# Seven block products per group of an expert: three of them made a group later, the fourth corner added in PSUM, and the first expert's operands built over two earlier blocks

## The chip, the cores and the metric

The kernel runs on one core of one Trainium2 chip. The metric is the device time of one execution in microseconds (us): 1494.73 us is the median of three runs of the kernel before (1494.47 to 1494.83).

## What is computed

Eight sequences of 1856 rows go through an attention-like layer, and its 14848 result rows of 256 numbers through a layer of 16 experts, of which each row takes one. Per row the router picks the best of four groups and the best of four experts in it; the expert is two matrix products with a ReLU between them, 256 to 1024 and back to 256 numbers, and the result is scaled by the product of two softmax weights.

```python
for e in range(Eg):
    h = np.maximum(xg[mask_e] @ w1[g, e], 0.0)
    ye = h @ w2[g, e]
    out[tok_idx] = combined[:, None] * ye
```

## The kernel before

Every matrix product is made from three products of rounded operands: a value is split into a high part (a copy in the matmul's format, made by ScalarE) and a low part (value minus high part, made by VectorE, often through the helper `lows`, L1172), and low times high, high times high and high times low are added up in PSUM.

The first part (until about 800 us) is the attention and the routing; the rows are sorted by expert into a table in device memory. The experts are then taken in order of their number of rows. The first four ("old" experts) run in twelve blocks of at most 512 rows (loop at L1314, `blocks`): `phase1` (L784) makes the 1024 hidden numbers as eight tiles of 128, `phase2_t` (L848) the result; the last two blocks, of 256 and of 512 rows, belong to the fourth expert.

The other twelve experts (loop at L1372) have their rows cut into two halves of w rows, w falling from 512 to 424 with the expert (and 448 for the last). Their first product is made by a block scheme: with both matrices cut in two by two, seven block products and some sums stand for eight block products. `duo_phase1` (L1257) makes four groups g of 128 hidden numbers, and in each the products 1 to 7, each of three matmuls of w columns. Per group:

- Products 1 and 2 go to a bank X (three banks take turns: x0, p0, x0, p1), product 5 to bank W; products 6, 7 and 4 to Y, product 3 to Z (two of Y and of Z, by the group's parity).
- After 1 ScalarE copies X to Y (L1289), after 5 it copies W to a tile in SBUF, `m5_w` (L1292).
- After 6 VectorE writes Z = Y + m5 (L1294). Product 7 then adds on Y, so it waits until this sum has read Y.
- After 7 VectorE makes the fourth corner C22 = Y + m5 in an SBUF tile `c22_w` (L1299). Product 4 adds on Y, so it waits until this has read Y.
- The four corners leave by `evict` (L1277): ScalarE writes the ReLU's high part (L1283), VectorE the low part (L1284, a scalar_tensor_tensor).

The order of the products is written out (L1306 to L1309) and TensorE follows it as written:

```python
seq += [(g, 1), (g, 5)] + [(g - 1, 4)] * (g > 0) + [(g, 6), (g, 2)] + [(g - 1, 3)] * (g > 0) + [(g, 7)]
```

The other engines' orders come from a planner that places the instructions by modelled times, earlier program order first; what is wrapped in `pin` stays behind the instruction that was written just before it on the same engine. Each engine then runs its queue in that order. A tile takes a buffer of its pool when its first writer runs; pool `vb` has 18 buffers, `at` three (L97, L103).

After the products of an expert its result is made in two halves, 48 matmuls each (`phase2_t`, L869). Into these matmuls are woven: the last two products (of the fourth group, 4 and 3, at slots 6 and 9), the "chores" (L1394), which build the next expert's operands (`split_w1` L1174, `split_duo` L1224, loads of weights by SyncE's queue), one each third matmul in the first half and each second in the second, and, late in the second half (slots 12, 14, 18, 20), the next expert's first four products. GpSimd splits the second weight (`split_w2`, L1192) during the products and sends the result rows to memory (L897). Result tiles that were still to be scaled and sent (`unsent`, `finish` L886) are taken up at every third product.

For the first of the twelve (expert 4) there is no expert before it, so its operands are built around the last old block: `split_w1` after that block's `phase1` (L1349), `split_duo` in the middle of its `phase2_t` (L1362). The weight's parts are the tiles p, a, s, t; a, s, t lie in pool `at`, which also holds the old experts' first weight. r0 to r5 are raw operands, r2 and r3 first hold sums of the weight's blocks and are then overwritten by `split_duo` with sums of the rows' blocks; x0 to x6 are the rows' high and low parts. `duo_banks` (L1249) writes four matmuls with the old weight into the Y and Z banks ahead of the first product. The steps of an "overflow" plan (`plan`, L1043, tiles `ov_...`) are strewn over blocks and products, on VectorE.

Of the kernel before, what the change touches and what calls it, by code (L numbers as in the profile page):

```python
# [19 lines left out]
P = 128  # L20
# [9 lines left out]
def tile_glu_attn_moe(  # L30
# [1118 lines left out]
    wst = {}  # L1149

    def duo_tiles():
        role = ["r0", "r1", "x5", "x6", "r2", "r3", "w0", "w1", "w2", "w3", "r4", "r5", "p", "x0", "x1", "x2", "x3", "x4"]
        for r in role:
            wst[r] = (new_vraw if r[0] == "r" else new_vb)(f"duo_{r}")
        for a in ("a", "s", "t"):
            wst[a] = new_at(f"duo_{a}", F32R)
# [17 lines left out]
    def split_w1():  # L1174
# [3 lines left out]
        s1, s3, s2, s4 = r2[:, 0:FH], r2[:, FH:F], r3[:, 0:FH], r3[:, FH:F]  # L1178
        yield pin(nc.vector.tensor_sub(out=s3, in0=a11, in1=a21))
        pin(nc.scalar.copy(out=wst["p"][:, 0:FH], in_=a11))  # L1180
        yield nc.vector.tensor_add(out=s1, in0=a21, in1=a22)
        nc.scalar.copy(out=wst["a"][:, 0:F], in_=r1)
        yield nc.vector.tensor_sub(out=s2, in0=s1, in1=a11)
        nc.scalar.copy(out=wst["s"][:, 0:F], in_=r2)
        yield nc.vector.tensor_sub(out=s4, in0=a12, in1=s2)
        nc.scalar.copy(out=wst["t"][:, 0:F], in_=r3)
        yield lows(wst["p"][:, FH:F], a11, wst["p"][:, 0:FH])
        yield lows(wst["a"][:, F:2 * F], r1, wst["a"][:, 0:F])
        yield lows(wst["s"][:, F:2 * F], r2, wst["s"][:, 0:F])
        yield lows(wst["t"][:, F:2 * F], r3, wst["t"][:, 0:F])  # L1190
# [33 lines left out]
    def split_duo(e):  # L1224
# [11 lines left out]
        nc.scalar.copy(out=wst["x0"][:, both], in_=r5[:, both])  # L1236
        yield nc.vector.tensor_sub(out=r2[:, two], in0=r5[:, two], in1=r4[:, two])
        nc.scalar.copy(out=wst["x3"][:, both], in_=r2[:, both])
        yield nc.vector.tensor_sub(out=r3[:, one], in0=r5[:, two], in1=r2[:, one])
        yield nc.vector.tensor_sub(out=r3[:, two], in0=r5[:, one], in1=r3[:, one])  # L1240
        nc.scalar.copy(out=wst["x5"][:, both], in_=r3[:, both])
        yield lows(wst["x2"][:, 512:512 + w], r4[:, one], wst["x2"][:, one])
        yield lows(wst["x4"][:, both], r2[:, both], wst["x3"][:, both])
        yield lows(wst["x1"][:, both], r5[:, both], wst["x0"][:, both])
        yield lows(wst["x6"][:, both], r3[:, both], wst["x5"][:, both])
# [11 lines left out]
    def duo_phase1(e):  # L1257
# [8 lines left out]
        def product(g, m):  # L1266
# [30 lines left out]
            elif m == 7:  # L1297
                t = sb("zm", [P, 512], F32, 2, f"c22_w{e}_{g}")[:, 0:w]
                nc.vector.tensor_add(out=t, in0=Y, in1=tmp[g])  # L1299
                evict(t, g + NF // 2, 1)  # L1300
            elif m == 3:
                evict(Z, g, 1)
            else:
                evict(Y, g + NF // 2, 0)

        seq = []  # L1306
        for g in range(NF // 2):
            seq += [(g, 1), (g, 5)] + [(g - 1, 4)] * (g > 0) + [(g, 6), (g, 2)] + [(g - 1, 3)] * (g > 0) + [(g, 7)]
        seq += [(NF // 2 - 1, 4), (NF // 2 - 1, 3)]  # L1309
# [4 lines left out]
    for i, (e, r0, n) in enumerate(blocks):  # L1314
# [21 lines left out]
        if e + 1 == NOLD and blocks[i - 1][0] != e:  # L1336
            duo_tiles()
# [176 lines left out]
```

## Time and profile before

| | |
|---|---|
| median of three runs | 1494.73 us |
| the profiled execution, its own time | 1498.23 us |
| its span (first to last instruction) | 1496.4 us |
| granted clock over the span, share of 2.4 GHz | 0.989 |
| TensorE busy | 1435.7 us (96%) |
| VectorE busy | 1253.7 us (84%) |
| ScalarE busy | 1015.7 us (68%) |
| GpSimd busy | 399.8 us (27%) |

Times below are us from the span's start. A matmul's busy time ends where its modelled end is, well after the next one has begun, so matmuls that follow each other closely leave no idle time, and the distance from start to start is their real pace. "Idle before" names the instruction whose end released the waiting one.

### The profile page before, as it was taken

Reading aid. Unit: us, or ns where it says so; the run is one execution under the profiler, and the core shown is the slowest. Engines: PE = TensorE matmul, PEld = TensorE weight load, DVE = VectorE, ACT = ScalarE, POOL = GpSimd, SP = SyncE. Lnnn points to the kernel's source line nnn. Section 1 sums busy time; section 2 is a strip of 40 time slices with the busy share of each in tenths; the row PEclk is TensorE's granted clock in tenths of the full one; section 3 lists DMA queues with packets and bytes.
Section 4 is the critical chain, followed back from the end, with each engine's and each line's share of the span. In section 5 each row is a group of like instructions: output and inputs, shape, how many; then the busy total and the mean of one; then the engine's idle time right before and its main releaser. Section 6 shows DMA issues by size and latency. Waiting matters only on the chain.

```text
span 1496.4 us, 22711 instructions
## 1 busy us (share of the span) xinstructions
PE 1435.7 (96%) x6981; PEld 1223.1 (82%) x6981; DVE 1253.7 (84%) x2460; ACT 1015.7 (68%) x1824; POOL 399.8 (27%) x462
## 2 busy tenths in 40 slices
PE   9999999999999999999999999879999999989996
PEld 7898888887888888887788989657777777878885
DVE  7889999989989999898996676697888987788883
ACT  8897787877878778787763444346666666666662
POOL 0002211222202221022223212144323344443343
PEclk9999999999999999999999999979999999999998
DMA  9988969889798997988864645415444344445441
GB/s 320 330 218 238 239 185 235 206 244 226 199 218 204 252 229 197 222 200 230 198 165 103 142 118 117 102 50 136 115 118 120 105 125 116 122 118 128 119 108 39
DMA packets 400045, 256.48 MB, mean 171 GB/s; under 512 B 244131, under 2 KB 355262, under 8 KB 399920
## 3 DMA queue, kind: packets, MB, share of 16 engines
q1 hardware_dynamic: 387984, 223.97, 60.4%
q0 software_dynamic: 11856, 30.90, 7.0%
q8 instruction: 55, 0.90, 0.3%
q14 instruction: 70, 0.57, 0.1%
q10 hardware_dynamic: 80, 0.13, 0.0%
HBM read 108.29 MB, written 89.21 MB: 132 GB/s over the span
## 4 chain that ended last, share of the span: by engine, by line
PE 71%; DVE 8%; issue 7%; DMA 6%; ACT 3%; POOL 3%; SPq 1%; DVEq 0%; ACTq 0%; POOLq 0%
PE o L403 12%; PE o L404 12%; PE o L406 11%; PE duo_p L869 10%; PE yT L869 6%; PE sc L366 4%; PE sc L367 4%; DMA yr_w<-yp_w 2%; PE ph L792 2%; PE ph L793 2%; PE ph L794 2%; PE duo_y L1275 2%; DVE hl_w L1284 2%; DMA out_dram<-y_w,meta_w 1%; POOL out_dram L897 1%
## 5 line engine op out<-in xcount | busy, mean ns | idle before, releaser
L403 PE MATMUL o<-ah,vl 128*128 128x512 f32 (+2 forms) x960 | 354.5, 370 | 0.6 <-DVE ah L378 0.4
L404 PE MATMUL o<-ah,vh 128*128 128x512 f32 (+2 forms) x960 | 354.3, 369 | 0.0
L406 PE MATMUL o<-al,vh 128*128 128x512 f32 (+2 forms) x896 | 329.1, 369 | 0.2 <-DVE al L356 0.2
L638 POOL DMA_INDIRECT bucket<-rows,di x121 | 137.5, 1136 | 376.1 <-issue 218.3
L370 ACT ACTIVATE r<-sc 128x512 f32<-128x512 f32 (+2 forms) x312 | 178.0, 571 | 66.8 <-PE sc L367 43.4
L403 PEld LDWEIGHTS o<-ah,vl 128*128 128x128 f32 x960 | 180.2, 188 | 30.6 <-DVE ah L378 0.8
L404 PEld LDWEIGHTS o<-ah,vh 128*128 128x128 f32 x960 | 180.2, 188 | 29.1
L381 DVE TENSOR_TENSOR al<-r,ah 128x512 fp32r<-128x512 f32 (+2 forms) x280 | 187.9, 671 | 17.3 <-DVE ah L378 0.5
L406 PEld LDWEIGHTS o<-al,vh 128*128 128x128 f32 x896 | 167.8, 188 | 27.2 <-DVE al L381 0.7
L869 PE MATMUL duo_p<-hh_w,duo_w 128*128 128x496 f32 (+9 forms) x692 | 182.9, 375 | 0.1
L377 ACT ACTIVATE r<-r 128x512 f32<-128x512 f32 (+2 forms) x284 | 173.9, 612 | 9.0
L869 PEld LDWEIGHTS duo_p<-hh_w,duo_w 128*128 128x128 f32 x692 | 129.8, 188 | 17.6 <-POOL duo_w L1199 0.5
L378 DVE CAST ah<-r 128x512 fp32r<-128x512 f32 (+2 forms) x284 | 116.9, 412 | 28.1 <-ACT r L377 22.8
L897 POOL DMA_INDIRECT out_dram<-y_w,meta_w x92 | 95.4, 1037 | 107.9 <-ACT y_w L896 90.9
L366 PE MATMUL sc<-zm,z2h 128*128 128x512 f32 (+2 forms) x312 | 120.5, 386 | 0.2 <-ACT r L370 0.2
L367 PE MATMUL sc<-zm,z2l 128*128 128x512 f32 (+2 forms) x312 | 118.9, 381 | 0.0
L869 PE MATMUL duo_p<-hl_w,duo_w 128*128 128x496 f32 (+9 forms) x346 | 105.3, 375 | 0.0
L306 DVE STREAM_TRANSPOSE mt<-r 128x512 f32<-128x512 f32 x147 | 103.7, 705 | 0.6
L356 DVE TENSOR_TENSOR al<-at,ah 128x512 fp32r<-128x512 f32 (+1 forms) x168 | 94.9, 579 | 1.2 <-ACT ah L355 1.1
L355 ACT CAST ah<-at 128x512 fp32r<-128x512 f32 (+1 forms) x168 | 86.1, 532 | 8.8 <-DMA at<-sym 4.7
L869 PE MATMUL yT<-hh,w_e 128*128 128x512 f32 (+6 forms) x384 | 82.4, 334 | 0.0
L888 DVE COPY y_w<-yr_w 128x512 uint16<-128x512 uint16 x92 | 47.5, 528 | 37.5 <-DMA yr_w<-yp_w 21.3
(239 smaller groups left out, 2893.5 us busy)
## 6 DMA issues: line engine op xcount, KB each, us to landing
sym<-mt SPq DMA_DIRECT2D x126, 256.0 KB
duo_r<-in_w_dram SPq DMA_DIRECT2D x48, 512.0 KB
at<-sym SPq DMA_DIRECT2D x84, 256.0 KB
bucket<-padrow SPq DMA_DIRECT2D x32, 660.0 KB
at<-sym SPq DMA_DIRECT2D x84, 160.0 KB
vr<-in_v_dram SPq DMA_DIRECT2D x23, 512.0 KB
ut<-in_uT_dram SPq DMA_DIRECT2D x23, 512.0 KB
raw_e<-in_w_dram SPq DMA_DIRECT2D x16, 512.0 KB
```

Source lines behind the costliest of these rows:

```text
L366: held(nc.tensor.matmul(ps[:, 0:w], z2h[:, ks], zm, start=True, stop=False))
L367: held(nc.tensor.matmul(ps[:, 0:w], z2l[:, ks], zm, start=False, stop=True))
L370: held(nc.scalar.activation(out=a, in_=ps[:, 0:w], func=AF.Relu, scale=1.0 / S))
L377: held(nc.scalar.activation(out=a, in_=a, func=AF.Square))
L378: held(nc.vector.tensor_copy(out=ah, in_=a))
L381: held(nc.vector.tensor_sub(out=al, in0=a, in1=f32(ah)))
L403: held(nc.tensor.matmul(o, vl[:, dsl], ah, start=(i == 0), stop=False))
L404: held(nc.tensor.matmul(o, vh[:, dsl], ah, start=False, stop=end and al is None))
L406: held(nc.tensor.matmul(o, vh[:, dsl], al, start=False, stop=end))
L638: nc.gpsimd.indirect_dma_start(out=views[(b * NQ + 2 * half + hs[h]) * NT + i], out_offset=bass.IndirectOffsetOnAxis(ap=di[0:n, i0 + i:i0 ...
L869: nc.tensor.matmul(o, wt["2"][f // 2][:, w0:w0 + P], hs[f][q // 2][:, 0:n], start=(at == 0), stop=(at == 3 * NF - 1))
L897: nc.gpsimd.indirect_dma_start(out=outs(), out_offset=bass.IndirectOffsetOnAxis(ap=meta[0:m, t, 1:2], axis=0), in_=y[0:m], in_offset=None, ...
```

## The change

- Product 7 of a group moves behind products 1 and 5 of the next group, product 4 behind that group's 6 and 2, in front of 3. After the last group come 7, 3, 4; the loop makes all but the last one ahead of the result's matmuls, and 4 goes to slot 4 of them.
- C22 is added into bank X of its own group, in PSUM, in place of an SBUF tile, and evicted from there.
- The operands of expert 4 are built earlier: seven of the eight steps of `split_w1` during `phase1` of the last but one old block, eight steps of `split_duo` during `phase1` of the last one, the rest right after it, before the last block's `phase2_t`.
- In `split_w1` the copies of p, a and s move one place forward, and that of t to just before its low part. In `split_duo` the low parts of x2 and x4 come before the second pair of sums, x6's and x0's steps after them, x1's last.
- The tiles are made when they are first asked for, and not all at once.
- `unsent` tiles are taken up only when fewer than 14 products are left; the chores of the first half begin at slot 6 (14 places for 16).

```diff
+        pin(nc.scalar.copy(out=wst["p"][:, 0:FH], in_=a11))
         yield pin(nc.vector.tensor_sub(out=s3, in0=a11, in1=a21))
-        pin(nc.scalar.copy(out=wst["p"][:, 0:FH], in_=a11))
+        nc.scalar.copy(out=wst["a"][:, 0:F], in_=r1)
         yield nc.vector.tensor_add(out=s1, in0=a21, in1=a22)
-        nc.scalar.copy(out=wst["a"][:, 0:F], in_=r1)
+        nc.scalar.copy(out=wst["s"][:, 0:F], in_=r2)
         yield nc.vector.tensor_sub(out=s2, in0=s1, in1=a11)
-        nc.scalar.copy(out=wst["s"][:, 0:F], in_=r2)
         yield nc.vector.tensor_sub(out=s4, in0=a12, in1=s2)
-        nc.scalar.copy(out=wst["t"][:, 0:F], in_=r3)
         yield lows(wst["p"][:, FH:F], a11, wst["p"][:, 0:FH])
         yield lows(wst["a"][:, F:2 * F], r1, wst["a"][:, 0:F])
         yield lows(wst["s"][:, F:2 * F], r2, wst["s"][:, 0:F])
+        nc.scalar.copy(out=wst["t"][:, 0:F], in_=r3)
         yield lows(wst["t"][:, F:2 * F], r3, wst["t"][:, 0:F])
...
         nc.scalar.copy(out=wst["x2"][:, one], in_=r4[:, one])
         yield nc.vector.tensor_sub(out=r2[:, one], in0=r4[:, two], in1=r4[:, one])
-        nc.scalar.copy(out=wst["x0"][:, both], in_=r5[:, both])
         yield nc.vector.tensor_sub(out=r2[:, two], in0=r5[:, two], in1=r4[:, two])
         nc.scalar.copy(out=wst["x3"][:, both], in_=r2[:, both])
+        yield lows(wst["x2"][:, 512:512 + w], r4[:, one], wst["x2"][:, one])
+        yield lows(wst["x4"][:, both], r2[:, both], wst["x3"][:, both])
         yield nc.vector.tensor_sub(out=r3[:, one], in0=r5[:, two], in1=r2[:, one])
         yield nc.vector.tensor_sub(out=r3[:, two], in0=r5[:, one], in1=r3[:, one])
         nc.scalar.copy(out=wst["x5"][:, both], in_=r3[:, both])
-        yield lows(wst["x2"][:, 512:512 + w], r4[:, one], wst["x2"][:, one])
-        yield lows(wst["x4"][:, both], r2[:, both], wst["x3"][:, both])
+        yield lows(wst["x6"][:, both], r3[:, both], wst["x5"][:, both])
+        nc.scalar.copy(out=wst["x0"][:, both], in_=r5[:, both])
         yield lows(wst["x1"][:, both], r5[:, both], wst["x0"][:, both])
-        yield lows(wst["x6"][:, both], r3[:, both], wst["x5"][:, both])
...
             elif m == 7:
-                t = sb("zm", [P, 512], F32, 2, f"c22_w{e}_{g}")[:, 0:w]
-                nc.vector.tensor_add(out=t, in0=Y, in1=tmp[g])
-                evict(t, g + NF // 2, 1)
+                nc.vector.tensor_add(out=X, in0=Y, in1=tmp[g])
+                evict(X, g + NF // 2, 1)
...
-            seq += [(g, 1), (g, 5)] + [(g - 1, 4)] * (g > 0) + [(g, 6), (g, 2)] + [(g - 1, 3)] * (g > 0) + [(g, 7)]
-        seq += [(NF // 2 - 1, 4), (NF // 2 - 1, 3)]
+            seq += [(g, 1), (g, 5)] + [(g - 1, 7)] * (g > 0) + [(g, 6), (g, 2)] + [(g - 1, 4), (g - 1, 3)] * (g > 0)
+        seq += [(NF // 2 - 1, m) for m in (7, 3, 4)]
...
+        if i + 2 == NB:
+            first = {"w1": split_w1()}
+
+        def mid_duo(f):
+            mid(f)
+            if i + 2 == NB and f:
+                next(first["w1"])
+            if last and f % 2:
+                for _ in range(2):
+                    next(first["x"])
+
+        hs = phase1(i, wts[e], x, n, mid_duo, False)
...
         if i + 2 == NB:
             duo_rows(NOLD)
+            first["x"] = split_duo(NOLD)
         if last:
-            for _ in split_w1():
+            for _ in first["w1"]:
                 pass
+            for _ in first["x"]:
+                pass
+            duo_w2(NOLD)
...
-            if last and t == 1:
-                duo_w2(NOLD)
-                for _ in split_duo(NOLD):
-                    pass
...
-        while len(prods) > 2:
+        while len(prods) > 1:
...
-            if unsent and len(prods) % 3 == 0:
+            if unsent and len(prods) < 14 and len(prods) % 3 == 0:
...
-        slots = {(0, 6): [tail[0]], (0, 9): [tail[1]]}
+        slots = {(0, 4): [prods[0]]}
         for d in range(ND):
-            for k in range(0, 24, 3):
+            for k in range(0 if d else 6, 24, 3):
                 slots.setdefault((d, k), []).append(chore(1))
```

## Rows read from the trace of the kernel before

**Rows 1.** The page, its first part: busy time and share of each engine.

```profile
PE 1435.7 (96%) x6981; PEld 1223.1 (82%) x6981; DVE 1253.7 (84%) x2460; ACT 1015.7 (68%) x1824; POOL 399.8 (27%) x462
```

**Rows 2.** The busy times in stretches (windows); columns in the first line.

```profile
core 0: us, PE busy (x) PEld busy (x) DVE busy (x) ACT busy (x) POOL busy (x), PEclk, DMA share, GB/s
...
962.00:993.00 31.00, 15.82 (x35) 10.11 (x36) 27.35 (x39) 9.45 (x14) 14.46 (x11) 0.61 0.32 80
...
1024.40:1441.80 417.40, 392.76 (x1801) 333.80 (x1800) 344.13 (x516) 262.59 (x476) 170.57 (x180) 1.00 0.47 119
...
1468.00:1496.40 28.40, 16.11 (x87) 14.32 (x85) 3.85 (x8) 5.58 (x12) 6.78 (x7) 0.85 0.22 47
```

**Rows 3.** The waits of TensorE from 950 us to the end.

```profile
PE duo_y L1275 <- DVE duo_z L1294: 21.7, 24, 2.0
...
PE duo_y L1275 <- DVE c_w L1299: 8.1, 9, 3.9
...
PE duo_x L1275 <- ACT duo_x L1234: 3.7, 1, 3.7
```

**Rows 4.** The timeline of TensorE at one wait: start, duration, what, idle before.

```profile
1247.96 0.80 PE L1275 MATMUL duo_z<-duo_x,duo_t 128*128 128x464 f32 x3
1250.56 0.90 PE L1275 MATMUL duo_y<-duo_x,duo_s 128*128 128x464 f32 x3 [1.79 <-DVE duo_z L1294]
1251.29 0.80 PE L1275 MATMUL duo_x<-duo_x,duo_p 128*128 128x464 f32 x3
1251.92 0.80 PE L1275 MATMUL duo_w<-duo_x,duo_s 128*128 128x464 f32 x3
```

**Rows 5.** The groups of instructions (lines) from 950 us, VectorE's.

```profile
L1284 DVE SCALAR_TENSOR_TENSOR hl_w<-c_w,hh_w 128x496 fp32r<-128x496 f32 (+9 forms) x36 | 50.5, 1404 | 17.4 <-ACT hh_w L1283 16.5 <-issue 0.6
...
L1284 DVE SCALAR_TENSOR_TENSOR h_w<-c_w,h_w 128x496 fp32r<-128x496 f32 (+9 forms) x12 | 8.8, 732 | 1.9 <-ACT h_w L1283 0.7
...
L1284 DVE SCALAR_TENSOR_TENSOR hl_w<-duo_y,hh_w 128x496 fp32r<-128x496 f32 (+9 forms) x48 | 30.4, 634 | 0.8 <-ACT hh_w L1283 0.8
...
L1299 DVE TENSOR_TENSOR c_w<-duo_y,m_w 128x496 f32<-128x496 f32 (+9 forms) x48 | 30.5, 635 | 1.0 <-PE duo_y L1275 0.5 <-issue 0.3
...
L1294 DVE TENSOR_TENSOR duo_z<-duo_y,m_w 128x496 f32<-128x496 f32 (+9 forms) x48 | 31.2, 649 | 19.5 <-PE duo_y L1275 16.7 <-ACT y_w L896 2.3 <-ACT hh_w L1283 0.4
```

**Rows 6.** The timeline of TensorE between the old blocks and the first products.

```profile
962.13 0.50 PE L1255 MATMUL duo_z<-w1h_e 128*128 128x512 f32 x1 [0.41 <-ACT yp L872]
...
966.33 1.22 PE L1275 MATMUL duo_x<-duo_x,duo_p 128*128 128x512 f32 x2 [3.70 <-ACT duo_x L1234]
...
987.62 1.65 PE L1275 MATMUL duo_y<-duo_x,duo_a 128*128 128x512 f32 x3 [3.92 <-DVE c_w L1299]
...
992.85 0.85 PE L1275 MATMUL duo_y<-duo_x,duo_s 128*128 128x512 f32 x3
```

**Rows 7.** The timeline of ScalarE there.

```profile
962.67 1.04 ACT L1186 CAST duo_t<-duo_r 128x1024 fp32r<-128x1024 f32 x1 [0.59 <-PE duo_z L1255]
```

**Rows 8.** The timeline of VectorE there, and one row ahead of it.

```profile
935.34 1.34 DVE L771 COPY xf<-xp 128x2048 uint16<-128x2048 uint16 x1
...
963.74 1.23 DVE L1172 TENSOR_TENSOR duo_t<-duo_r,duo_t 128x1024 fp32r<-128x1024 f32 x1 [8.12 <-ACT duo_t L1186]
...
964.89 2.60 DVE L1228 COPY duo_r<-xp_w 128x1024 uint16<-128x1024 uint16 x4
...
967.38 0.67 DVE L1235 TENSOR_TENSOR duo_r<-duo_r 128x512 f32<-128x512 f32 x1
...
980.24 3.16 DVE L1111 TENSOR_TENSOR ov_it<-ov_it 128x64 f32<-128x64 f32 x1
```

**Rows 9.** The busy times in the last two old blocks, and in one expert's second part.

```profile
927.50:941.00 13.50, 13.50 (x107) 13.12 (x107) 11.06 (x27) 5.91 (x13) 4.58 (x4) 1.00 0.61 109
...
941.00:953.50 12.50, 12.50 (x56) 10.20 (x55) 8.86 (x17) 5.97 (x10) 4.30 (x5) 1.00 0.24 62
...
1218.60:1239.10 20.50, 20.21 (x96) 17.53 (x95) 19.09 (x29) 12.24 (x19) 1.92 (x3) 1.00 0.42 104
```

More of the change, by code (lines that the diff above doesn't have):

```diff
@@ L1147, in tile_glu_attn_moe, with __missing__ @@
     planned = plan()
[L1149 to L1156, printed above, removed]
+    class Duo(dict):
+        def __missing__(self, k):
+            new = new_vraw if k[0] == "r" else new_vb if k[0] in "xwp" else lambda name: new_at(name, F32R)
+            self[k] = new(f"duo_{k}")
+            return self[k]
+    wst = Duo()
     def duo_w1(e):
@@ L1336, in tile_glu_attn_moe @@
         if e + 1 == NOLD and blocks[i - 1][0] != e:
-            duo_tiles()
             duo_w1(NOLD)
-        hs = phase1(i, wts[e], x, n, mid, False)
+        if i + 2 == NB:
[8 more added lines that the diff above has]
+        hs = phase1(i, wts[e], x, n, mid_duo, False)
         if i + 1 == NEARLY:
@@ L1374, in tile_glu_attn_moe @@
         build2 = split_w2()
-        at = len(prods)
-        while len(prods) > 2:
+        while len(prods) > 1:
             next(build2, None)
@@ L1379, in tile_glu_attn_moe @@
                 next(planned, None)
-            if unsent and len(prods) % 3 == 0:
+            if unsent and len(prods) < 14 and len(prods) % 3 == 0:
                 unsent.pop(0)()
             if more and len(prods) == 8:
-                for _ in build2:
-                    pass
                 duo_w1(e + 1)
@@ L1387, in tile_glu_attn_moe @@
             prods.pop(0)()
-        for _ in build2:
-            pass
-        work = []
+        work = ()
         if more:
-            hs2, prods2 = [], []
             def chores():
@@ L1399, in tile_glu_attn_moe @@
             work = chores()
-        tail = prods
-        half_p = [(0, 6)], [(0, 9)]
-        slots = {(0, 6): [tail[0]], (0, 9): [tail[1]]}
         def chore(n):
             return lambda: [next(work, None) for _ in range(n)] if more else None
+        slots = {(0, 4): [prods[0]]}
         for d in range(ND):
-            for k in range(0, 24, 3):
+            for k in range(0 if d else 6, 24, 3):
                 slots.setdefault((d, k), []).append(chore(1))
```

## The prediction

> **What bounds the kernel now.** I read the page's first part, then busy time in stretches, then TensorE's waits, then the timelines around the largest of them. TensorE is busy 96% of the span [rows 1], so at best the other 4%, and time in which it runs slowly, can be won. The stretches say where that lies [rows 2]: in the ten middle experts TensorE is idle 417.40 - 392.76 = 24.6 us of 417; between the last old block and expert 4's products 15.2 of 31 us, with the granted clock at 0.61, so part of the busy time there is at the lower of the clock's two levels; and in the last 28.4 us, after the last product, which the change hardly touches. The waits put names to it [rows 3]: product 7 waits for the sum Z = Y + m5 24 times, 21.7 us; product 4 for the sum C22 nine times, 8.1 us; what is left is the start of expert 4, where ScalarE's copy of x2 comes 3.70 us late [rows 6].
>
> A wait costs more than its row says. Three matmuls of 464 columns take 0.63 us (1251.29 to 1251.92, [rows 4]). The product at 1250.56 should have begun at 1247.96 + 0.63 = 1248.59, so it is 1.97 late where the row says 1.79, and the next one begins 0.73 instead of 0.63 after it: 2.07 in all, 0.28 over the row.
>
> Why the sums are late, the groups of instructions tell [rows 5]. In one group VectorE makes two sums and four low parts. At 0.634 us each (five of the six forms lie between 0.634 and 0.649) that is 3.8 us in 7 x 0.63 = 4.4 us of TensorE's time, which fits. But C22's low part takes 1.404 us in 36 of its 48 instances; then it is 4.6 us, and VectorE falls behind in every group. Both inputs of this one lie in SBUF; the other low parts read PSUM. In the fourth groups, the 12 others, it takes 0.732. GpSimd splits weights during the products and is nearly idle after them (1.92 of 20.5 us, [rows 9]), so I read the extra 0.77 us as VectorE waiting for GpSimd at SBUF.
>
> **The change part by part.**
>
> *Products 7, 4 and 3 later.* Between 6 and 7 of a group now lie 2, 4, 3, 1, 5 in place of 2 and 3: three products more, 1.9 us, against a longest wait of 2.0 us [rows 3]. Between 7 and 4 lie 6 and 2 where 1 and 5 lay: no more room than before. Between 6 and 3 there is still nearly a whole turn. What can be won is 21.7 + 8.1, less the 3.92 that belongs to expert 4's start [rows 6]: 25.9 in 32 waits, and 32 x 0.28 = 9.0 beside it, 34.9 us.
>
> *C22 in PSUM.* The sum goes from SBUF to PSUM as Z does: 0.635 to 0.649, 48 x 0.014 = 0.7 us more. Its low part then has the form of the others: 36 x (1.404 - 0.634) = 27.7 and 12 x (0.732 - 0.634) = 1.2 us less. VectorE wins 28.2 us, none of it on the path by itself; it is what makes the sum come in time for product 4, which got no more room. The bank X now stays taken until C22 is evicted, and the group after next begins in it: from the sum's end two more steps of 0.634 against two products of slack, a wait of 0 to 0.5 us in one group of an expert, since only x0 comes round within one. A rule speaks against this. By the rows, a low part out of PSUM is no dearer: 0.634 against 0.732 [rows 5]. The Trainium skill, Perfetto Trace Analysis, section Optimizing Scalar/DVE Operations, gives some 60 ns of access overhead per VectorE instruction on SBUF and some 125 on PSUM; by that VectorE would get back 48 x 0.065 = 3 us of its 28, and the forecast would stand.
>
> *Left over in the twelve experts.* Nothing before shows the new waits. Lower bound 0. Upper bound: product 4's waits stay, 4.2 us in eight of the nine plus 8 x 0.28, and the chores, which now begin at slot 6 and so up to six matmuls (1.3 us) later, are late for the next expert's first products by that much in eleven experts, 14 us: 20 in all. That danger is real: in the second part of an expert VectorE is busy 19.09 of 20.50 us [rows 9]. Against it, VectorE now leaves the products without a backlog, and x1, the last operand made, is for the fourth product. I take 6, half a microsecond per expert: 34.9 - 6 = **29 us won**.
>
> *Expert 4's start.* A matmul of 512 columns takes 0.23 us (0.63 / 3 x 512 / 464, [rows 4]). From the end of the last one into the Z bank (962.13 + 0.23) to 992.85 eleven products ran [rows 6]: 33 x 0.23 = 7.6 us of work in 30.5, 22.9 lost. The chain [rows 7, 8]: t's copy waits until the old weight's buffer is free (962.67), its low part follows (963.74), and the row copies L1228, pinned behind it, begin at 964.89; all of x0 to x6 comes after. With the change p, a, s, the row copies, x2, x3 and x4 come out of the last two old blocks, x0 and x1 need only r5 and can come before 962, and products 1 and 5 start at once. But t still waits for 962.67, and r3, which t's low part reads, is what `split_duo` overwrites to make x5 and x6. So product 6 waits for: t's copy 1.04, its low part 1.23 (until 964.97), two sums of 0.67 (966.3), x5's copy 1.04 (967.4), x6's low part 1.23 (968.7; a copy and a low part of that width, priced by t's). Products 1 and 5 end at 963.7, so 6 begins 3.7 us late and its third matmul a second time: 4.9 us. After an idle stretch of 3.70 us the clock was at the lower level before, and after 3.92 the matmuls ran at half pace until 992.85, 5.2 us [rows 2, 6]. I count 2 us for that (between 0 and 2.6). The overflow plan runs on VectorE in that very stretch (one step took 3.16 us, [rows 8]) and is not moved: 0 to 6, I take 3.
>
> *The two old blocks.* They get some 3.9 us of VectorE's work (four steps of 0.67 and a low part of 1.23; a's and the first sum's place can be earlier) in a block where it has 2.4 free, and 5.8 (2.60 for the row copies, three steps of 0.67, 1.23) where it has 3.6 and 2 us of sums leave [rows 8, 9]. The second fits. In the first, the copy that joins the last block's rows (935.34, pinned) slips, and TensorE, without a gap there, waits for it: 0 to 3.5, I take 2. Lost in all 4.9 + 2 + 3 + 2 = 12 of 22.9: **11 us won**.
>
> *At no cost.* `unsent` tiles later: nothing in the products reads them, and GpSimd's weight splits go ahead of their sends, so the result's matmuls find their weights earlier; without that cover a late split would hold the first of them. m5 of two groups lives at once now, and the pool that it shared with C22's tile has the two buffers for it. SyncE: `duo_w2` of expert 4 is issued half a block earlier; its r0 and r1 have been read by then, so it does not hold the block's transposes behind it. The weight splits on GpSimd still wait for the old block's buffers. ScalarE makes as many copies and ReLUs as before and is busy 68% [rows 1].
>
> **The sum.** 1498.23 - 29 - 11 = 1458; that execution's span is 1496.4 and the 1.8 around it stay; the runs' median, 1494.73, lies 3.5 us below it, so 1455 us.
>
> **The rivals.**
> 1. *Everything goes as drawn* (0.60): 1455, between 1445 and 1465.
> 2. *The waits vanish whole* (0.13): no left-over, no plan, no slip: 34.9 + 22.9 - 4.9 = 53 us, 1498.2 - 53 - 3.5 = 1442. For it: VectorE's 28 us; against it, VectorE's 93% in an expert's second part [rows 9].
> 3. *VectorE becomes the bound* (0.13): its queue keeps half of the 34.9, and expert 4's start gives 5: 1498 - 22.5 - 3.5 = 1472.
> 4. *The eviction stays at 1.4 us* (0.07), because its length has another cause than where C22 lies; the change then doesn't do what it says in this part. Product 7 wins by its distance, product 4 keeps its 8.1 + 9 x 0.28 = 10.6: 34.9 - 10.6 - 6 + 11 = 29 us, 1498.2 - 29 - 3.5 = 1466.
> 5. *Slower* (0.04): VectorE's queue, laid out by modelled times, has C22's sum behind the low part of the next group's product 2. Product 4 follows that 2 directly and would wait for a ReLU, a low part and the sum, some 3 x 0.634 = 1.9 us, in 3 groups of 12 experts: 68 us less 40 won, 1495 + 28 = 1523. It decides from 40 / 36 = 1.1 us per group. Against it: 7 comes two products before 2, so the sum is ready first.
>
> The remaining 0.03 is no change. Faster or slower by 0.2%, 3 us, is about what a measurement of this kernel can tell. Faster: 0.60 + 0.13 + 0.13 + 0.07 = 0.93; same 0.03; slower 0.04. The range reaches from rival 2 to rival 3: 1442 to 1473.
>
> **What would show it.** Right: TensorE's waits for Z gone from its list; C22's low part at 0.63 us; products of expert 4 from about 962.5 with one stop before product 6 that ends with x5 and x6; about 38 us from expert to expert at 464 columns. Wrong: waits of product 4 for C22, or of product 2 or 6 for VectorE's low parts, in every expert; TensorE idle between the last two old blocks; a clock below 1.00 after expert 4's start.

## The result and the profile after

The changed kernel takes 1471.87 us (median of four runs, 1469.22 to 1473.58) against 1494.78 for the kernel before on the same chip: ratio 0.9844, 95% interval 0.9827 to 0.9861, 22.9 us faster. The profiled execution took 1471.43 us with a span of 1469.6. The two profiled executions differ by 26.8 us. That splits at three landmarks: the first matmul of the last but one old block, where the change begins, the start of the twelfth product of expert 4, and the start of the last matmul of a product:

```
us                                before   after   won   forecast
up to the last but one old block  927.46   925.59   1.9     0
from there to the 12th product     65.39    55.69   9.7    11
12th to last product              474.61   459.18  15.4    29
last product to the end            28.94    29.14  -0.2     0
```

The first 1.9 us are not shown to be the change's: the edits begin behind that mark, and it lies between 922.5 and 928.2 in the eleven profiled executions with the early operands and between 926.5 and 928.4 in the three without. So the start of expert 4 gave nearly what was drawn and the steady part gave half. The page's first part, then the stretches that answer to [rows 2] (busy us of each engine, clock, DMA):

```profile
PE 1428.8 (97%) x6981; PEld 1229.3 (84%) x6981; DVE 1231.9 (84%) x2460; ACT 1020.1 (69%) x1824; POOL 394.0 (27%) x462
```

```profile
962.00:981.30 19.30, 10.36 (x28) 7.03 (x28) 16.93 (x24) 6.38 (x10) 12.65 (x9) 0.65 0.30 85
1016.00:1419.80 403.80, 390.17 (x1801) 339.89 (x1800) 329.64 (x520) 266.90 (x477) 162.54 (x178) 0.99 0.48 123
```

The ten middle experts take 403.8 us instead of 417.4 with the same 1801 matmuls; TensorE is still idle 13.6 us of them, and the clock is no longer 1.00. TensorE's waits in place of [rows 3] (us in total, times, longest):

```profile
PE duo_y L1274 <- ACT duo_y L1288: 8.3, 11, 1.8
PE duo_y L1274 <- ACT duo_x L1241: 5.9, 1, 5.9
PE duo_p L869 <- POOL duo_w L1198: 3.6, 1, 3.6
PE duo_y L1274 <- DVE duo_p L1297: 3.4, 3, 1.8
PE duo_y L1274 <- DVE duo_x L1171: 1.9, 1, 1.9
```

Code lines lie one lower than before. The waits for Z are gone. In the steady part three others have come: product 6 for ScalarE's X to Y copy (L1288), the second phase for GpSimd's split of the second weights (L1198), product 4 for C22 (L1297). The second and the fifth line are expert 4's start. C22's low part, [rows 5], in VectorE's groups:

```profile
L1283 DVE SCALAR_TENSOR_TENSOR hl_w<-duo_p,hh_w 128x496 fp32r<-128x496 f32 (+9 forms) x36 | 23.1, 641 | 0.5 <-ACT hh_w L1282 0.5
L1283 DVE SCALAR_TENSOR_TENSOR h_w<-duo_p,h_w 128x496 fp32r<-128x496 f32 (+9 forms) x12 | 7.6, 632 | 0.0
```

The lines go by bank, so the first counts product 2's low parts in p0 and p1 with C22's of one group; C22's of the two groups in x0's bank stand with product 2's there, at 0.64. C22's low part is as cheap as the rest. The start of expert 4 against [rows 6 to 8]: TensorE, ScalarE and VectorE in their timelines.

```profile
967.74 1.22 PE L1274 MATMUL duo_y<-duo_x,duo_t 128*128 128x512 f32 x2 [5.93 <-ACT duo_x L1241]
970.90 0.79 PE L1274 MATMUL duo_y<-duo_x,duo_t 128*128 128x512 f32 x1 [1.94 <-DVE duo_x L1171]
```

```profile
961.90 1.05 ACT L1188 CAST duo_t<-duo_r 128x1024 fp32r<-128x1024 f32 x1
966.65 1.04 ACT L1241 CAST duo_x<-duo_r 128x1024 fp32r<-128x1024 f32 x1 [3.70 <-DVE duo_r L1240]
```

```profile
963.81 1.21 DVE L1171 TENSOR_TENSOR duo_t<-duo_r,duo_t 128x1024 fp32r<-128x1024 f32 x1
...
965.92 0.69 DVE L1240 TENSOR_TENSOR duo_r<-duo_r,duo_r 128x512 f32<-128x512 f32 x1
967.42 1.23 DVE L1093 TENSOR_TENSOR ov_big<-ov_le,ov_it 128x1024 f32<-128x1024 f32 x1 [0.80 <-POOL duo_w L1197]
968.56 2.29 DVE L1171 TENSOR_TENSOR duo_x<-duo_r,duo_x 128x1024 fp32r<-128x1024 f32 x1
```

t's copy, its low part, the two sums over r3, x5's copy: the chain of the prediction. Product 6 begins at 967.7 for 967.4, but this execution was 1.9 us ahead when the change began, so it is some 2 us later than drawn. Products 1 and 5 ran inside the old block, before the last matmul into the Z bank (961.42), so they fill nothing of this wait; and a row's copy (963.46) and a row's weighting (964.94) stand among VectorE's steps of the chain. Behind it a plan step (L1093) stands ahead of x6's low part.

**Where the steady part loses.** Twelve times after expert 4's start product 6 comes over 0.3 us late for the copy, 10.4 us in all by start-to-start times. One such place, ScalarE:

```profile
1192.78 0.51 ACT L896 ACTIVATE y_w<-y_w,meta_w 128x256 f32<-128x256 f32 x1
1193.48 0.55 ACT L1291 COPY m_w<-duo_w 128x472 f32<-128x472 f32 x1 [0.18 <-PE duo_w L1274]
1193.93 0.56 ACT L1288 COPY duo_y<-duo_p 128x472 f32<-128x472 f32 x1
```

L896 weights a result row for a send. Behind it the queue has m5's copy, which waits for product 5, ahead of Y's copy, which needs only product 1; product 6 begins at 1194.54, 0.7 late. Seven of the twelve are like this. In three others, the two dearest among them, a send's weighting and the second phase's evictions stand ahead; ScalarE, then VectorE:

```profile
1263.15 0.51 ACT L896 ACTIVATE y_w<-y_w,meta_w 80x256 f32<-80x256 f32 x1 [1.96 <-DVE y_w L888]
1263.56 0.78 ACT L872 COPY yp_w<-duo_p 128x768 uint16<-128x768 uint16 x1
...
1264.43 0.54 ACT L1288 COPY duo_y<-duo_p 128x456 f32<-128x456 f32 x1
```

```profile
1262.61 0.46 DVE L888 COPY y_w<-yr_w 80x512 uint16<-80x512 uint16 x1 [2.29 <-DMA out_dram<-y_w,meta_w]
```

VectorE's copy of the row waits until an earlier send has left its buffer, ScalarE's weighting waits for VectorE, the X to Y copy for ScalarE, and product 6 for the copy. In all twelve a weighting is among the four ScalarE instructions ahead of the copy.

### The profile page after: what moved, and what is told of

Its sections match the earlier page's. It is cut to its first block, busy times and chain, and to the rows that moved or that the text cites. A ratio compares the mean times of both kernels' runs of the same rounds, so it can differ in the third digit from the quotient of the medians.

```text
span 1469.6 us, 22695 instructions
## 1 busy us (share of the span) xinstructions
PE 1428.8 (97%) x6981; PEld 1229.3 (84%) x6981; DVE 1231.9 (84%) x2460; ACT 1020.1 (69%) x1824; POOL 394.0 (27%) x462
## 4 chain that ended last, share of the span: by engine, by line
PE 78%; DVE 10%; issue 5%; DMA 2%; POOL 2%; ACT 2%; SPq 0%; DVEq 0%; ACTq 0%; POOLq 0%
PE o L403 13%; PE o L404 13%; PE o L406 12%; PE duo_p L869 11%; PE yT L869 5%; PE duo_y L1274 4%; PE sc L366 4%; PE sc L367 4%; PE ph L792 2%; PE duo_x L1274 2%; PE ph L793 2%; PE ph L794 2%; PE duo_w L1274 2%; PE duo_p L1274 1%; PE duo_z L1274 1%
## 5 line engine op out<-in xcount | busy, mean ns | idle before, releaser
L406 PEld LDWEIGHTS o<-al,vh 128*128 128x128 f32 x896 | 167.9, 188 | 26.9 <-DVE al L381 0.7
L897 POOL DMA_INDIRECT out_dram<-y,meta x37 | 40.9, 1105 | 130.8 <-DVE y L894 124.9
```

The lines of the kernel that those rows point to most:

```text
L406: held(nc.tensor.matmul(o, vh[:, dsl], al, start=False, stop=end))
L897: nc.gpsimd.indirect_dma_start(out=outs(), out_offset=bass.IndirectOffsetOnAxis(ap=meta[0:m, t, 1:2], axis=0), in_=y[0:m], in_offset=None, ...
```

## The experiments

Each ran at least five times, beside the kernel before on the same chip; chips differ (the kernel before has medians from 1493.75 to 1498.33 us), so the ratios are compared. "Steady" is the time from the twelfth product of expert 4 to the last one, in the profiled execution.

```
                         ratio   95% interval     steady us
changed kernel           0.9844  0.9827 - 0.9861  459.2  (before 474.6)
1  PSUM alone            0.9996  0.9985 - 1.0008  473.6
2  PSUM and order        0.9889  0.9871 - 0.9907  458.6
3  sends early           0.9850  0.9831 - 0.9868  456.9
4  x5 in r4              0.9782  0.9764 - 0.9800  459.1
5  C22 in SBUF           0.9893  0.9876 - 0.9910  467.7
6  weighting on VectorE  0.9891  0.9876 - 0.9905  468.6
7  weighting on GpSimd   1.0023  1.0011 - 1.0035  481.4
8  3 ahead of 6          1.0022  1.0009 - 1.0035  492.1
9  no sends between      0.9736  0.9722 - 0.9749  446.2
10 plan later            0.9830  0.9817 - 0.9844  464.6
11 sends behind 6        0.9810  0.9797 - 0.9824  460.4
12 weighting split       0.9908  0.9889 - 0.9928  478.1
```

**1. C22 in PSUM alone.** In the kernel before:

```
-                t = sb("zm", [P, 512], F32, 2, f"c22_w{e}_{g}")[:, 0:w]
-                nc.vector.tensor_add(out=t, in0=Y, in1=tmp[g])
-                evict(t, g + NF // 2, 1)
+                nc.vector.tensor_add(out=X, in0=Y, in1=tmp[g])
+                evict(X, g + NF // 2, 1)
```

> The kernel before with one part of the change alone: C22 added in the PSUM bank X instead of in an SBUF tile; order of the products, sends and expert 4's start stay as before. Theory (the prediction's): VectorE's 1.4 us low parts of C22 are what makes the sums late, so product 7's 21.7 us of waits for Z and product 4's 8.1 us fall by more than half: 1480 us (1474 to 1485). Rival: the two products between 6 and 7 are too short a distance for the sum whatever VectorE's load is: the waits for Z stay above 15 us and the time is 1489 us or more. In both the low part of C22 takes 0.63 us.

No change at all, though VectorE's busy time falls from 1253.7 [rows 1] to 1231.6 us. TensorE's waits, then VectorE and TensorE at one of them:

```profile
PE duo_y L1275 <- DVE duo_x L1298: 14.7, 13, 4.3
PE duo_y L1275 <- DVE duo_z L1294: 5.8, 8, 1.5
PE duo_y L1275 <- DVE duo_p L1298: 5.0, 4, 1.4
```

```profile
1298.21 2.15 DVE L888 COPY y_w<-yr_w 80x512 uint16<-80x512 uint16 x1
1300.26 0.62 DVE L1284 SCALAR_TENSOR_TENSOR hl_w<-duo_x,hh_w 128x456 fp32r<-128x456 f32 x1
1300.80 0.61 DVE L1284 SCALAR_TENSOR_TENSOR hl_w<-duo_z,hh_w 128x456 fp32r<-128x456 f32 x1
1301.34 0.62 DVE L1298 TENSOR_TENSOR duo_x<-duo_y,m_w 128x456 f32<-128x456 f32 x1
```

```profile
1302.02 0.68 PE L1275 MATMUL duo_y<-duo_x,duo_a 128*128 128x456 f32 x2 [1.84 <-DVE duo_x L1298]
```

The waits for Z fell as the theory said, 21.7 to 5.8, and those for C22 rose from 8.1 to 19.7: C22's sum stands in VectorE's queue behind a result row's copy and two low parts, and two products later product 4 wants it. The copy, 0.46 us in the median, takes 2.15 here: now it is the instruction that runs beside GpSimd's subtraction, as C22's low part did before.

```profile
1298.73 1.31 POOL L1199 TENSOR_TENSOR duo_w<-duo_r,duo_w 128x512 fp32r<-128x512 f32 x1
```

At most of the other late products 4 the copies take their 0.45 us, and the queue alone makes the sum late. Less work did not help a sum that is queued behind others.

**2. PSUM and order.** The first experiment's kernel with the change's order, tail slots and chores; sends and early operands as before.

```
-            seq += [(g, 1), (g, 5)] + [(g - 1, 4)] * (g > 0) + [(g, 6), (g, 2)] + [(g - 1, 3)] * (g > 0) + [(g, 7)]
+            seq += [(g, 1), (g, 5)] + [(g - 1, 7)] * (g > 0) + [(g, 6), (g, 2)] + [(g - 1, 4), (g - 1, 3)] * (g > 0)
```

> The kernel before with C22 in PSUM and with the new order of the products (7, 4 and 3 in the next group's turn), but with expert 4's start as before and with the sends of result rows still taken at every third product from 24 left on instead of from 12 left on. Theory 1 (the later sends cost: their steps stand ahead of the X to Y copy on ScalarE): no wait of product 6 for the X to Y copy above 1 us in all, so before less the changed kernel's 15 us beyond expert 4's start and less some 8 more: 1471 us (1467 to 1475). Theory 2 (the new order itself makes the copy late): 1480 us (1477 to 1483), with product 6 waiting 6 to 10 us.

1481.24 us, theory 2's number: beyond the first experiment the order gives 1.1%, and with C22 in PSUM the whole steady gain is here.

```profile
PE duo_y L1275 <- ACT duo_y L1289: 9.3, 12, 1.8
PE duo_x L1275 <- DVE hl_w L1284: 5.3, 9, 0.7
```

The copy's waits are as large with the old places of the sends.

**3. Sends early.**

```
-            if unsent and len(prods) < 14 and len(prods) % 3 == 0:
+            if unsent and len(prods) % 3 == 0:
```

> The changed kernel with one condition taken out: sends of result rows are taken at every third product from 24 left on, as before, not from 12 left on. Theory 1: the 0.67 us waits of product 6 for the X to Y copy, one in nearly every expert, and the one late weight split on GpSimd (3.8 us and 2.4 us of half clock behind it) go: 1472 - 8 to 14 = 1461 us (1458 to 1465). Theory 2 (order itself): 1472 us, within 3. Theory 3: the early sends collide with the second group's copies instead: the same waits at another place, 1472 us or up to 6 more.

Theory 3: the same ratio as the changed kernel. The waits move; product 1 now waits for the low part that still holds its bank, and GpSimd's late split is gone:

```profile
PE duo_y L1274 <- ACT duo_y L1288: 9.1, 12, 1.7
PE duo_x L1274 <- DVE hl_w L1283: 5.9, 10, 1.1
```

Against the second experiment the early operands are worth 0.0039, some 6 us. In expert 4's start the early sends cost: from the last but one old block to the twelfth product it takes 59.1 us here and 55.7 in the changed kernel, and product 4 waits there for C22, whose sum stands behind plan steps in VectorE's queue:

```profile
PE duo_y L1274 <- DVE duo_x L1297: 2.4, 1, 2.4
```

In the steady part the early sends give 2.3 us back.

**4. x5 in r4.**

```
-        yield nc.vector.tensor_sub(out=r3[:, one], in0=r5[:, two], in1=r2[:, one])
-        yield nc.vector.tensor_sub(out=r3[:, two], in0=r5[:, one], in1=r3[:, one])
-        nc.scalar.copy(out=wst["x5"][:, both], in_=r3[:, both])
-        yield lows(wst["x6"][:, both], r3[:, both], wst["x5"][:, both])
+        yield nc.vector.tensor_sub(out=r4[:, one], in0=r5[:, two], in1=r2[:, one])
+        yield nc.vector.tensor_sub(out=r4[:, two], in0=r5[:, one], in1=r4[:, one])
+        nc.scalar.copy(out=wst["x5"][:, both], in_=r4[:, both])
+        yield lows(wst["x6"][:, both], r4[:, both], wst["x5"][:, both])
```

> The changed kernel with the two sums behind x5 and x6 written over r4, which is free once x2's low part is made, instead of over r3, which t's low part still reads. Theory (the prediction's chain at expert 4's start: t copy, t low part, sums, x5 copy, x6 low part): product 6 begins with t's low part, 965.1 instead of 967.7, and no longer waits for x6, so 2.6 + 1.9 us and perhaps 1 to 2 us of half clock: 1467 us (1465 to 1469). Rival: t's low part and the overflow plan on VectorE hold product 6 and 2 anyway: 1471 us or more.

1466.42 us, ratio 0.9782; its interval lies wholly below the changed kernel's, and it is the fastest kernel here that leaves nothing out. x5's copy now runs inside the last old block; ScalarE, then VectorE and TensorE:

```profile
956.41 1.06 ACT L1241 CAST duo_x<-duo_r 128x1024 fp32r<-128x1024 f32 x1 [2.74 <-DVE duo_r L1240]
```

```profile
964.93 1.21 DVE L1171 TENSOR_TENSOR duo_t<-duo_r,duo_t 128x1024 fp32r<-128x1024 f32 x1
```

```profile
966.20 1.65 PE L1274 MATMUL duo_y<-duo_x,duo_t 128*128 128x512 f32 x3 [3.27 <-DVE duo_t L1171]
```

Product 6 waits for t alone and its three matmuls run together. From the last but one old block to the twelfth product (976.20) it takes 49.5 us instead of 55.7; the steady part is the same. The reuse of r3 was 6 us of the start.

**5. C22 in SBUF.** The changed kernel:

```
-                nc.vector.tensor_add(out=X, in0=Y, in1=tmp[g])
-                evict(X, g + NF // 2, 1)
+                nc.vector.tensor_add(out=tmp[g], in0=Y, in1=tmp[g])
+                evict(tmp[g], g + NF // 2, 1)
```

> The changed kernel with one part undone: C22 is added in SBUF, over m5, as before outside PSUM; order, sends and early start stay. Theory 1 (VectorE's 28 us count once the order gives each sum three products of room, and only then): the low part takes 1.4 us again in three groups of four, VectorE's sums come late for product 4, 2 and 6, and 10 to 20 us of the changed kernel's 23 are lost: ratio to before 0.991 to 0.998. Theory 2 (the distance alone was the cause; VectorE has room enough even with 1.4 us): ratio 0.983 to 0.987, as the changed kernel.

0.9893, just short of theory 1's range: PSUM is worth 0.0049, 7 us, once the order has changed. That is not the price of the old 1.4 us: the low part averages 0.86 us here:

```profile
L1283 DVE SCALAR_TENSOR_TENSOR hl_w<-m_w,hh_w 128x496 fp32r<-128x496 f32 (+9 forms) x36 | 31.0, 860 | 0.0
```

**6. Weighting on VectorE.** The fourth experiment's kernel; each row's weighting behind its copy on the same engine.

```
-            if isinstance(name, int):
-                nc.vector.tensor_scalar(out=y[0:m], in0=y[0:m], scalar1=cw, scalar2=None, op0=ALU.mult)
-            else:
-                nc.scalar.activation(out=y[0:m], in_=y[0:m], func=AF.Copy, scale=cw)
+            nc.vector.tensor_scalar(out=y[0:m], in0=y[0:m], scalar1=cw, scalar2=None, op0=ALU.mult)
```

> The fourth experiment's kernel (x5 in r4, ratio 0.978) with the weighting of the result rows, 88 ScalarE instructions of 0.51 us, moved to VectorE behind the copy that makes those rows. Theory 1 (that ScalarE instruction, which waits for VectorE's copy, holds the X to Y copy back: it is one of the four instructions ahead of every late copy): product 6's waits for the copy fall from 6 to under 2 us and the ratio to 0.972 (0.969 to 0.975); VectorE pays 88 x 0.35 us out of the time that the change freed. Theory 2 (VectorE is the bound again with 31 us more): new waits for its sums and low parts, ratio 0.980 or more.

Theory 2 (92 instructions moved, not 88). The copy's waits shrink only to 4.6 us, and C22's sum is late for product 4:

```profile
PE duo_y L1271 <- DVE duo_p L1294: 15.4, 10, 2.5
PE duo_y L1271 <- ACT duo_y L1285: 4.6, 7, 1.0
```

**7. Weighting on GpSimd.**

```
-                nc.scalar.activation(out=y[0:m], in_=y[0:m], func=AF.Copy, scale=cw)
+                nc.gpsimd.tensor_scalar(out=y[0:m], in0=y[0:m], scalar1=cw, scalar2=None, op0=ALU.mult)
```

> The fourth experiment's kernel with the weighting of the result rows moved from ScalarE to GpSimd, right ahead of the send. Theory 1: as in the sixth experiment the waits for the X to Y copy go, and VectorE pays nothing: ratio 0.971 (0.968 to 0.975). Theory 2: GpSimd, which sends, splits the second weights and now scales as well, is late with the split oftener than once (3.6 us each, with half clock behind it) or holds VectorE back: ratio 0.979 or more.

Theory 2: GpSimd is busy only 33%, and its split is late in nearly every expert. Two of the eleven waits fall behind the last product, where it takes 41.4 us to the end instead of the fourth experiment's 30.7.

```profile
PE duo_p L869 <- POOL duo_w L1198: 26.2, 11, 5.0
```

**8. Product 3 ahead of 6.**

```
-            seq += [(g, 1), (g, 5)] + [(g - 1, 7)] * (g > 0) + [(g, 6), (g, 2)] + [(g - 1, 4), (g - 1, 3)] * (g > 0)
+            seq += [(g, 1), (g, 5)] + [(g - 1, 7), (g - 1, 3)] * (g > 0) + [(g, 6), (g, 2)] + [(g - 1, 4)] * (g > 0)
```

> The fourth experiment's kernel with product 3 of the group before moved ahead of product 6: 1, 5, 7', 3', 6, 2, 4'. The X to Y copy then has three products of room after product 1 in place of two, and C22's sum still two before product 4. Theory 1 (0.6 us of room more takes all waits of 0.5 to 0.7 us away): waits for the copy under 3 us, ratio 0.975 (0.973 to 0.977). Theory 2 (Y's bank, which product 4 now leaves one product before product 1's copy overwrites it, sets the copy's time): the waits stay or grow, ratio 0.978 or more.

Neither: the copy's waits fall to 3.7 us, and one other wait costs far more.

```profile
PE duo_y L1274 <- DVE duo_p L1297: 26.5, 12, 3.0
```

All twelve are at one place, the last product 4 of an expert, at slot 4 of the second phase. By start-to-start times it is 28.4 us late there in the twelve experts, against 3.9 in the changed kernel, 17.0 in the sixth and 17.9 in the twelfth experiment. The tail of the list was not edited; what moved is where VectorE's queue has C22's last sum. Between the end of product 7 and that sum stood mostly one low part in the changed kernel; here it is three to eight instructions, low parts, rows' copies and weight sums.

**9. No sends between products.**

```
             if unsent and len(prods) < 14 and len(prods) % 3 == 0:
-                unsent.pop(0)()
+                unsent.pop(0)
```

> The changed kernel without the sends that are taken between the products: the copy on VectorE, the weighting on ScalarE and the send on GpSimd of those result rows, up to four tiles of 128 an expert, are left out. Theory 1 (they hold the X to Y copy and the last weight split back): product 6's waits for the copy, 8.3 us and some 0.35 us for each of the eleven beside it, and GpSimd's late split, 3.6 and 2.4 us of half clock, are gone: 14 to 18 us, ratio to before 0.974 (0.972 to 0.976). Theory 2 (the order of the products itself leaves ScalarE too little room): product 6 still waits 5 us or more, ratio 0.979 or more.

Theory 1's number: 0.0108 below the changed kernel, 16 us, of which the steady part shows 13.0, with the clock at 1.00 there. The seven waits behind m5's copy are gone, and GpSimd's late split too. The four copy waits that stay are of the dear kind, behind a send taken in the second phase:

```profile
PE duo_y L1274 <- ACT duo_y L1288: 5.4, 4, 2.0
```

**10. Plan later.**

```
-            if len(prods) % 4 == 0:
+            if e > NOLD and len(prods) % 4 == 0:
```

> The changed kernel with the six steps of the overflow plan that VectorE does in expert 4's products put off to the products of the next experts. The prediction counted 3 us (0 to 6) for them. Theory 1: x6's and x1's low parts no longer stand behind a plan step of 1.2 us each, so product 6's third matmul and product 2's come 1.2 us earlier each: 2 to 4 us, ratio 0.982 (0.981 to 0.983). Theory 2: VectorE has room enough there, or the steps cost as much where they go: ratio 0.984 or more.

Ratio 0.983 as theory 1 has it, but the interval overlaps with the changed kernel's, and from the last but one old block to the last product it takes 514.3 us here and 514.9 there: no gain is shown. Inside, both theories hold. Product 6's three matmuls run together, and the stretch to the twelfth product takes 49.7 us instead of 55.7:

```profile
963.63 2.05 PE L1274 MATMUL duo_y<-duo_x,duo_t 128*128 128x512 f32 x3 [4.97 <-ACT duo_x L1241]
```

But the second stretch of 84 matmuls of products behind that takes 47.2 instead of 42.3.

**11. Sends behind 6.** The fourth experiment's kernel:

```
-            if unsent and len(prods) < 14 and len(prods) % 3 == 0:
+            if unsent and len(prods) in (20, 13, 6, 3):
```

> The fourth experiment's kernel (ratio 0.978) with the four sends between the products at 20, 13, 6 and 3 left instead of 12, 9, 6 and 3: each right behind a product 6, which is the furthest from the next X to Y copy. Theory 1 (the weighting ahead of the copy holds it back, so its place decides): the 0.5 to 0.7 us waits of product 6, most of 6.1 us, go, and with earlier sends GpSimd's late split (3.6 us and 1.6 of half clock): ratio 0.973 (0.970 to 0.975). Theory 2 (each queue's order is laid out by modelled times, and a send in another place makes other sums late): new waits of product 4 or 1 in place of the old, ratio 0.977 or more.

Theory 2: 0.981. The copy's waits stay (7.2 us, 12 times), product 4's for C22 nearly go, and product 1's for the low part in its bank come:

```profile
PE duo_x L1274 <- DVE hl_w L1283: 6.8, 8, 1.3
```

**12. Weighting split.** The fourth experiment's kernel; `finish` takes a flag.

```
-            if isinstance(name, int):
+            if vector or isinstance(name, int):
...
-                unsent.pop(0)()
+                unsent.pop(0)(True)
```

> The fourth experiment's kernel (ratio 0.978) with the weighting moved to VectorE only for the sends taken between the products, where VectorE is busy some 0.8 of the time; those in the second phase, where it is busy 0.95 and where the sixth experiment lost, stay on ScalarE. Theory 1 (a result row's weighting ahead of the X to Y copy is what delays it in the last group, and VectorE has room between the products): the waits of 0.5 to 0.9 us at product 6 go where a send between products stood ahead, some 8 of the 10, the late split on GpSimd stays or gets shorter: ratio 0.974 (0.972 to 0.976). Theory 2 (any work added to VectorE in that stretch delays C22's sum, as in the sixth experiment): product 4's waits grow past 6 us, ratio 0.980 or more.

Theory 2. VectorE and TensorE at one tail product 4:

```profile
1163.81 0.68 DVE L1183 TENSOR_TENSOR duo_r<-duo_r,duo_r 128x512 f32<-128x512 f32 x1
1164.41 0.65 DVE L1283 SCALAR_TENSOR_TENSOR hl_w<-duo_z,hh_w 128x480 fp32r<-128x480 f32 x1
1164.98 0.45 DVE L888 COPY y_w<-yr_w 112x512 uint16<-112x512 uint16 x1
1165.32 0.67 DVE L1297 TENSOR_TENSOR duo_p<-duo_y,m_w 128x480 f32<-128x480 f32 x1
```

```profile
1166.04 0.49 PE L1274 MATMUL duo_y<-duo_x,duo_a 128*128 128x480 f32 x1 [1.81 <-DVE duo_p L1297]
```

The sum has its input since product 7 ended, before 1163, yet comes behind a weight sum, a low part and a row's copy. In the fourth experiment one low part stands there; the only edit since is the rows' weighting on VectorE (0.34 us just before, at 1162.42), so it is what moved the sum.

## Why the prediction was right and where it was wrong

The sign and the range held, but 1471.87 lies 17 us above the forecast and 1 us inside the range, while the four runs spread over 4: that the range held is partly luck. Of the 17 us the steady part makes 13.6, expert 4's start 1.3 and the level of the two executions 2.0 (3.9 by their distance from their medians, less the 1.9 before the change begins).

- **Expert 4's start: the total nearly right, the parts not.** 9.7 us were won for 11. Against the matmuls' full pace (0.23 us at 512 columns) the stretch lost 23.7 us before and loses 14.0 now, where 12 were forecast. The mis-sized term is the plan: without its steps (tenth experiment) 8.0 are lost, so it costs 6.0, the upper end, where I took 3. In those 8.0 the stops at product 6 make 5.6 (forecast 4.9) and half clock 1.8 (forecast 2); the slip of the two old blocks is some 0.4 (forecast 2). That the chain over r3 holds product 6 is shown by the fourth experiment. Nor is the gain all of the early operands: in the kernel before, the first, second and third experiments and the changed kernel the stretch takes 65.4, 65.1, 63.3, 59.1 and 55.7 us. Added in this order, PSUM and order give 2.1, the early operands 4.2 and the later sends 3.4; in another order the shares may differ.
- **C22 in PSUM: size right, use wrong.** The low parts together take 27.9 us less, where 28.9 were forecast. VectorE's busy time fell by 21.8 only, because other work got longer, the rows' copies by 3.9. But "it is what makes the sum come in time for product 4" failed: alone it gave nothing (first experiment), and with the new order 7 us. The read cause, VectorE behind in every group through the 1.4 us, held only for Z; C22's sum was late by its place in the queue and, at some places, by a row's copy that waits for a send or runs beside GpSimd.
- **The order: right.** With C22 in PSUM it wins the steady 15 us (second experiment against the first). 1, 5 and 7' between the products of a chain give room for Z, whose waits are gone. With C22 in SBUF the steady part gains 7.0 of the 15.4 (fifth experiment), and PSUM alone gave 1.0: most of the gain needs both.
- **Left over: the step that failed.** I took 6 us and it is 34.9 - 15.4 = 19.5, at the bound of 20, and not for the reasons that made that bound. Late chores did not show. Product 6 for the copy 10.4, product 4 at the tail 3.9, GpSimd's split 3.8 and half clock behind three of these waits 5.7 are 23.8 us; the kernel before lost some small times beside my 34.9 (41 us in all at full pace), most of which went too. I had asked what VectorE would be late with next, and passed over ScalarE with a count of its instructions and its 68%. The copy it makes between products 1 and 6 has two products of room, as it had before; that the waits for Z had hidden this is argued, not shown.
- **At no cost: two items fell.** The later sends have a price and a gain: against the third experiment they win 3.4 us in expert 4's start and lose 2.3 in the steady part. And I named the cover of GpSimd's split and that a late one would hold the result's matmuls. It happened once: in expert 14 a send, waiting for ScalarE's weighting, stood ahead of the last split.

```profile
1399.17 2.19 POOL L897 DMA_INDIRECT out_dram<-y_w,meta_w  x1 [2.43 <-ACT y_w L896]
1401.38 1.28 POOL L1198 TENSOR_TENSOR duo_w<-duo_r,duo_w 128x512 fp32r<-128x512 f32 x1
```

- **The 3.5 us to the median: not a property of the kernel.** The profiled execution of before lay 3.5 above its median, that of the changed kernel 0.4 below its own.
- **The rivals.** Rival 3's time came, by another engine's queue than VectorE's alone. Rival 5's wait did not come where it was put: product 4 behind the next group's 2 is on time in the steady part (0.2 us late once). The same mechanism, C22's sum queued behind low parts with product 4 close behind it, is real at the tail: it cost 17 to 28 us in the sixth, eighth and twelfth experiments and costs 3.9 in the changed kernel.
- **The signs.** Of those for right, the waits for Z are gone and C22's low part takes 0.64 us; from expert to expert at 464 columns it takes 39.3 us (42.5 before), where 38 was named. Of those for wrong, one came: the clock behind expert 4's start is 0.99.

That about half of the remaining loss, 13.0 of the 26.9 us that the steady part takes beyond full pace, comes through the sends between the products is shown by the ninth experiment; it also leaves their own work out, so the 16 us are an upper bound of what better places could give. A version that keeps the sends and wins that was not found: three ways of moving them or their weighting (sixth, seventh, twelfth) lost, and one (eleventh) was no better than the fourth.

## What to carry to other kernels

A wait that goes lays open the next link of its chain, on whatever engine that is: for each product write down what must happen before it, on every queue, and the room it has, before a gain is counted whole. How much an engine is busy says little where the place of one instruction in its queue decides; a relieved engine gave nothing until the order gave its sums room. Where queues are laid out by modelled times, an edit at one place can move an instruction at another, so after each edit look up where the tight ones stand.

## What was not expected of the hardware

**The 1.4 us depend on GpSimd.** In the kernel before, of the 36 dear low parts the 23 that ran mostly beside GpSimd's subtraction L1199 took 1.74 us in the mean, up to 3.34; the two beside nothing took 0.69. In the changed kernel, nine low parts out of bank p0 or p1 beside that subtraction (there L1198) took 0.64. The prediction read the pairing so; that it reaches nearly five times the length was new. With GpSimd idle the two forms cost the same: eight instances each, of mixed widths, took 0.66 us out of PSUM (changed kernel) and 0.66 out of SBUF (fifth experiment). The Trainium skill, Perfetto Trace Analysis, section Optimizing Scalar/DVE Operations, has PSUM some 65 ns dearer; these runs show no such difference.

**Equal waits, unequal clock.** Three stretches behind waits of 1.78, 1.73 and 1.80 us; the granted clock is the third number from the right:

```profile
995.50:998.50 3.00, 3.00 (x8) 2.32 (x9) 3.00 (x5) 2.04 (x4) 0.00 (x0) 0.53 0.00 0
1265.20:1268.20 3.00, 3.00 (x15) 2.73 (x16) 2.18 (x4) 2.18 (x5) 2.14 (x3) 1.00 0.51 115
1343.80:1346.80 3.00, 3.00 (x9) 2.69 (x9) 1.35 (x3) 1.16 (x3) 2.11 (x3) 0.50 0.50 109
```

At 0.50, the lower level of 1.2 GHz, 9 matmuls run in the time of 15. So a wait of 1.8 us cost up to 1.7 us more behind it, or nothing; what decides was not tried. After expert 4's start, the waits of before, all up to 2.0 us, were followed by at most three slow matmuls, 0.36 us.
